# Linear attention and a SoLU feed-forward on one core: chunk 0 in token halves, and an order of work read from a table

## The chip, the cores and the metric

The kernel runs on one core of a Trainium2 chip. The metric is device microseconds of one execution, from which the median of several runs is taken. Profiles are of one further execution by the hardware profiler; their span runs from the first to the last instruction. PE is TensorE, DVE VectorE, ACT ScalarE, POOL GpSimd, SP SyncE.

## What is computed

For 8 batches of 8 heads, 576 tokens and 64 columns per head (fp32 inputs), linear attention without a softmax, then a root-mean-square norm per head; then a feed-forward with 512 inputs, 1024 hidden columns and a SoLU (h times its softmax, layer-normed):

```python
kv = np.einsum('bhsd,bhse->bhde', k, v)
out = np.einsum('bhsd,bhde->bhse', q, kv)
rms = np.sqrt(np.mean(out * out, axis=-1, keepdims=True) + 1e-06)
x = (out / rms * g_norm)          # heads side by side: 4608 tokens x 512
h = x @ w_in
sm = softmax(h)                   # over the 1024 columns, +1e-9 in the sum
solu = h * sm
ln = (solu - mean(solu)) / np.sqrt(var(solu) + 1e-06) * g_ln
return ln @ w_out                 # 4608 x 512, fp32
```

## The kernel before, in words

**Chunks.** The 4608 tokens go in nine chunks of 512. Chunk c below 8 holds tokens 0 to 7 of each run of nine tokens of batch c (a batch is 64 partitions by nine tokens); chunk 8 holds the ninth token of all eight batches, for which q_last (L235) is loaded.

**Attention of a chunk.** k, v and q are cast to bf16 by loads from POOL's queue (L225). For batches 0 and 1 each load is cut into two halves of heads, for the others it is whole. kv_mm (L279) forms k'v on PE, copies put it into kvd in two row arrangements (L298). q is transposed on PE (qT_mm, L312, and a copy) for chunks 0 to 3, and by a DMA transpose from SP's queue for chunks 4 to 8 (q_turn, L329). o_mm (L336) gives q times kv in two PSUM tiles; each is squared (o_sq L360, for one tile of chunk 0 a DVE copy and a POOL product, L352 to L358), averaged over the head on PE (s_mm, L366), turned into 1/rms on ACT (in chunk 0 by a reciprocal square root, L380; later by Ln and Exp, L370 and L374, in another table of ACT functions, loaded once at L394), and multiplied in (x_mul, L386). So a chunk has four quarters (half hf, tile z); in the kernel before, half hf of chunk 0 means four of the eight heads.

**Feed-forward of a chunk.** h_mm (L466) makes eight groups of four matmuls with 512 columns, one per 128 hidden columns; each needs all four quarters of x. Exp goes to ACT (L474), u = h times exp to DVE (L481), u squared to POOL or ACT (u_sq, L488), the sum of two exps to POOL (e_sum, L497). sums (L526) adds u, u squared and the exps over the hidden columns on PE; a transpose and a few small DVE operations and two of ACT give one factor per token (rstd, L558). out_mm (L579) multiplies u by w_out, which is first centred (w_mean L565, w_center L573), in four token blocks of two groups; scale (L613) applies the factor, store (L626) writes out. In chunk 8 the last block is cut into two halves of columns (L588 to L611), and each block is stored by two DMAs of 64 rows.

**Order.** Every piece of work is given to Plan (L19) with an engine, a length, a rank, what it needs, and the buffers that it opens and uses; order (L42) then picks, again and again, the piece that could start first by these lengths, the lower rank first. This fixes each engine's instruction order; on the chip every engine works its list strictly in order. PSUM's eight banks are dealt into five pools that rotate (L136): two for h, two for out, two for o, one for s, one for the rest. Engines are fixed by rules (for instance L295, L515, L615). POOL's loads of batches 5 to 7 wait in the plan until the transpose of the batch before has been given out ("turned", L256), and the plan charges a transpose that meets a busy load queue 12.0 instead of 3.5 (L81 to L84):

```python
if n[0] == "qT" and engine == "sp":

    if queue > t - 2.0:
        length, queue = 12.0, queue + 2.2
```

At most eight DMAs of POOL's queue are outstanding; the next one waits for the one eight places earlier. Matmuls on zeros (warm, L207) fill PE's first 18 us.

## Time and profile before

| what | value |
|---|---|
| median of 3 runs | 192.51 us (192.28 to 195.38) |
| span of the profiled execution | 191.5 us |
| PE busy | 178.6 us, 93% of the span |
| ACT, POOL, DVE busy | 141.2, 128.5, 122.5 us |
| granted TensorE clock, mean | 0.998 |
| loads on POOL's queue | 17.30 MB written, q0 |
| stores and transposes, SP's and ACT's queues | 11.68 MB, q1 |

The timeline lists instructions in the order of time: start, duration, engine, line, operation, destination <- sources, and in brackets how long the engine idled before it and what ended that. A row may merge several of the same kind (x4). Matmul durations contain the pipeline, so that rows overlap: a group of four is listed with about 1.03 us and occupies 0.86. A row of SP, ACTq or POOL with DMA in it is the issue of the transfer, not the transfer.

### The profile page before, as it was taken

Reading aid. Unit: us, or ns where it says so; the run is one execution under the profiler, and the core shown is the slowest. Engines: PE = TensorE matmul, PEld = TensorE weight load, DVE = VectorE, ACT = ScalarE, POOL = GpSimd, SP = SyncE. Lnnn points to the kernel's source line nnn. Section 1 sums busy time; section 2 is a strip of 40 time slices with the busy share of each in tenths; the row PEclk is TensorE's granted clock in tenths of the full one; section 3 lists DMA queues with packets and bytes.
Section 4 is the critical chain, followed back from the end, with each engine's and each line's share of the span. In section 5 each row is a group of like instructions: output and inputs, shape, how many; then the busy total and the mean of one; then the engine's idle time right before and its main releaser. Section 6 shows DMA issues by size and latency. Waiting matters only on the chain.

```text
span 191.5 us, 5356 instructions
## 1 busy us (share of the span) xinstructions
PE 178.6 (93%) x2218; PEld 88.5 (46%) x2218; DVE 122.5 (64%) x241; ACT 141.2 (74%) x245; POOL 128.5 (67%) x136
## 2 busy tenths in 40 slices
PE   7989796999799999999999999999999999999980
PEld 2343355554245554554455446445444544544550
DVE  1445679386866878577686758586676847565350
ACT  2026897879898899989888897989787796555330
POOL 7953499600799886796897996698387646854200
PEclk9999999999999999999999999999999999999999
DMA  3999999999995599699999999448824022414435
GB/s 49 179 197 259 364 208 209 204 209 258 249 207 86 119 167 249 168 178 229 219 152 232 243 149 174 107 49 159 98 55 103 14 55 68 99 33 96 93 74 145
DMA packets 35607, 29.70 MB, mean 155 GB/s; under 512 B 16504, under 2 KB 30080, under 8 KB 35584
## 3 DMA queue, kind: packets, MB, share of 16 engines
q0 software_dynamic: 19088, 17.30, 54.9%
q1 hardware_dynamic: 16176, 11.68, 26.8%
q10 hardware_dynamic: 320, 0.39, 0.6%
q8 instruction: 17, 0.28, 0.6%
q14 instruction: 6, 0.05, 0.1%
HBM read 32.51 MB, written 9.44 MB: 219 GB/s over the span
## 4 chain that ended last, share of the span: by engine, by line
PE 72%; DMA 11%; POOL 5%; ACT 5%; DVE 3%; issue 1%; ACTq 1%; POOLq 0%
PE out_ps L583 28%; PE h_ps L469 28%; DMA v_sb<-in_v_dram 11%; PE misc_ps L535 5%; PE s_ps L368 3%; PE o_ps L347 2%; POOL usq_sb L495 2%; DVE x_sb L389 2%; ACT rst_sb L376 2%; PE misc_ps L290 1%; POOL k_sb L230 1%; ACT lss_sb L372 1%; PE misc_ps L210 1%; DVE u_sb L484 1%; PE o_ps L583 1%
## 5 line engine op out<-in xcount | busy, mean ns | idle before, releaser
L469 PE MATMUL h_ps<-x_sb,w_in_sb 128*128 128x512 bf16 x276 | 70.5, 379 | 2.3 <-DVE x_sb L389 1.1
L583 PE MATMUL out_ps<-w_out_sb,u_sb 128*128 128x512 bf16 x272 | 69.4, 379 | 0.0
L495 POOL TENSOR_TENSOR usq_sb<-u_sb 128x512 bf16<-128x512 bf16 x50 | 51.8, 1041 | 23.0 <-DVE u_sb L484 22.9
L484 DVE TENSOR_TENSOR u_sb<-h_ps,e_sb 128x512 bf16<-128x512 f32 x69 | 47.4, 687 | 25.7 <-ACT e_sb L477 24.9
L501 POOL TENSOR_TENSOR es_sb<-e_sb 128x512 bf16<-128x512 f32 x36 | 45.8, 1274 | 19.7 <-ACT e_sb L477 19.4
L477 ACT ACTIVATE e_sb<-h_ps,zero_t 128x512 f32<-128x512 f32 x69 | 47.0, 681 | 9.2 <-PE h_ps L469 8.7
L469 PEld LDWEIGHTS <-w_in_sb 128*128 128x128 bf16 x288 | 27.0, 98 | 35.6 <-issue 5.4
L583 PEld LDWEIGHTS <-u_sb 128*128 128x128 bf16 x280 | 26.4, 98 | 31.2 <-issue 1.0
L389 DVE SCALAR_TENSOR_TENSOR x_sb<-o_ps,g_rep,rst_sb 128x512 bf16<-128x512 f32 x32 | 23.9, 748 | 11.6 <-ACT rst_sb L376 11.6
L618 DVE TENSOR_SCALAR ob_sb<-out_ps,rstd 128x512 f32<-128x512 f32 x33 | 24.6, 746 | 6.9 <-PE out_ps L583 4.4
L362 ACT ACTIVATE osq_sb<-o_ps,zero_t 128x512 bf16<-128x512 f32 x31 | 20.0, 680 | 12.2 <-PE o_ps L347 12.2
L372 ACT ACTIVATE lss_sb<-s_ps,eps_t 128x512 f32<-128x512 f32 x32 | 22.1, 689 | 2.4 <-PE s_ps L368 2.3
L376 ACT ACTIVATE rst_sb<-lss_sb,zero_t 128x512 f32<-128x512 f32 x32 | 23.1, 723 | 0.8
L493 ACT ACTIVATE usq_sb<-u_sb,zero_t 128x512 bf16<-128x512 bf16 x22 | 15.8, 718 | 9.1 <-DVE u_sb L484 9.0
L368 PE MATMUL s_ps<-osq_sb,head_mean 128*128 128x512 bf16 x34 | 12.9, 379 | 0.6 <-ACT osq_sb L362 0.6
L535 PEld LDWEIGHTS <-stat_sel 128*32 128x32 bf16 x720 | 10.1, 97 | 3.8 <-issue 3.8
L210 PE MATMUL s_ps<-zeros 128*128 128x512 bf16 x28 | 10.1, 488 | 1.4 <-DVE zero_t L175 1.2
L230 POOL DMA_DIRECT2D k_sb<-in_k_dram x10 | 7.7, 773 | 4.3 <-DMA w_in_sb<-in_moe_w_in_dram 2.8
L230 POOL DMA_DIRECT2D q_sb<-in_q_dram x10 | 7.5, 750 | 3.6 <-DMA w_in_sb<-in_moe_w_in_dram 1.4
L308 DVE CAST kvd<-misc_ps 64x128 bf16<-64x128 f32 (+1 forms) x24 | 6.9, 288 | 3.2 <-PE misc_ps L290 2.0
L290 PEld LDWEIGHTS <-k_sb 64*64 64x64 bf16 x576 | 7.5, 107 | 3.2 <-issue 3.2
L290 PE MATMUL misc_ps<-v_sb,k_sb 64*64 64x64 bf16 x360 | 7.8, 194 | 1.0 <-DMA v_sb<-in_v_dram 0.9
(85 smaller groups left out, 132.6 us busy)
## 6 DMA issues: line engine op xcount, KB each, us to landing
out_dram<-ob_sb SPq DMA_DIRECT2D x68, 128.0 KB, 3.1
k_sb<-in_k_dram POOLq DMA_DIRECT2D x6, 576.0 KB, 12.3
v_sb<-in_v_dram POOLq DMA_DIRECT2D x6, 576.0 KB, 12.6
q_sb<-in_q_dram POOLq DMA_DIRECT2D x6, 512.0 KB, 14.3
w_out_f<-in_moe_w_out_dram POOLq DMA_DIRECT2D x1, 2048.0 KB, 17.4
k_sb<-in_k_dram POOLq DMA_DIRECT2D x4, 288.0 KB, 12.4
v_sb<-in_v_dram POOLq DMA_DIRECT2D x4, 288.0 KB, 12.6
q_sb<-in_q_dram POOLq DMA_DIRECT2D x4, 256.0 KB, 12.5
```

The source lines that it names most:

```text
L362: nc.scalar.activation(out=t[:, :], in_=T[("o", *i)].rearrange("p a b c -> p (a b c)"), func=AF.Square, bias=zero_t[:, :])
L372: nc.scalar.activation(out=t[:, :], in_=T["s", i][:, :], func=AF.Ln, bias=eps_t[:, :])
L376: nc.scalar.activation(out=t.rearrange("p a b c -> p (a b c)"), in_=T["lss", i][:, :], func=AF.Exp, scale=-0.5, bias=zero_t[:, :])
L389: nc.vector.scalar_tensor_tensor(out=T["x", c][:, 2 * hf:2 * hf + 2, z], in0=T["o", c, hf, z][:, :, :, :], scalar=g_rep[:, :], in1=T["rst" ...
L469: nc.tensor.matmul(t[:, :], w_in_sb[:, dt, f * 128:(f + 1) * 128], T["x", c][:, dt].rearrange("p a b c -> p (a b c)"), start=(dt == 0), st ...
L477: nc.scalar.activation(out=T["e", c, f // 2][:, f % 2, :], in_=T["h", c, f][:, :], func=AF.Exp, bias=zero_t[:, :])
L484: nc.vector.tensor_tensor(out=T["u", c][:, f, :], in0=T["h", c, f][:, :], in1=T["e", c, f // 2][:, f % 2, :], op=MUL)
L495: nc.gpsimd.tensor_tensor(out=dst, in0=src, in1=src, op=MUL)
L501: nc.gpsimd.tensor_tensor(out=T["es", c][:, n, :], in0=e[:, 0, :], in1=e[:, 1, :], op=ADD)
L535: nc.tensor.matmul(T["sum", c][32 * j:32 * j + 32, 0, :], stat_sel[:, i, :], cols, start=(part == 0 and n == 0), stop=(part == 2 and n == ...
L583: nc.tensor.matmul(T["acc", c, m][:, :], T["u", c][:, f, m * 128:(m + 1) * 128], w_out_sb[:, f, :], start=(f == 0), stop=(f == NF - 1),)
L618: nc.vector.tensor_scalar_mul(out=t[:, :], in0=T["acc", c, m][:, :], scalar1=T["rstd", c][:, m:m + 1])
```

## The change

1. **An order from a table.** Plan no longer schedules. A string, ORDER, lists all pieces; each entry may name the engine (`@act`) and the slots of the buffers that the piece opens (`=2`). The eight PSUM banks become one pool, `ps`, any bank for any tile. The fused o_mm and kv_mm of the old plan are gone.
2. **Chunk 0 in halves of its tokens.** For chunk 0, half hf now means half of each head's tokens, for all heads: q of batch 0 is loaded in two token halves, transposes and o_mm go by token half (16 shorter matmuls instead of 8 per half), and h_mm, exp and u of chunk 0 are cut into 16 pieces of 256 columns; a piece needs two quarters of x instead of four.
3. **Last tokens placed for stores of 128 rows.** The batches of q_last are placed so that a block's 128 rows are two neighbouring batches, one DMA per block (and per column half in the last block).

```diff
+ORDER = """
+warm.0=7 v.0.0=0 k.0.0=0 warm.1=7 warm.2=7 kv_mm.0.0=0 kv.0.0.0@act kv.0.0.1@act kv.0.0.2@act k.0.1 v.0.1 warm.3=7
...
+    def emit(self, order):
...
+             fn(engine or engines[0])
...
-    banks = {"h": 2, "out": 2, "o": 2, "s": 1, "misc": 1}
...
+        "ps": 8, "k": 3, "v": 3, "q": 3, "qT": 3, "osq": 4, "lss": 2, "rst": 3, "oc": 1, "x": 2, "e": 4, "u": 2, "usq": 2,
...
+        if parts > 1 and (name, b) == ("q", 0):
+            at = slice(4 * part, 4 * part + 4)
...
-        behind = [] if b < 2 else [("h_mm", 0, 0)] if b == 2 else [("h_mm", b - 3, 2 if b == 3 else 0)] + ([("turned", b - 1)] if b - 1 in XBAR else [])
...
+    def h_mm(c, f, g):
+        t = T["h", c, f, g] = bank(("ps", "h", c, f, g), [128, 512 if g is None else 256], FP32)
+        for dt in range(NP):
+            nc.tensor.matmul(
+                t[:, :], w_in_sb[:, dt, f * 128:(f + 1) * 128], T["x", c][:, dt, cols_of(g)],
+                start=(dt == 0), stop=(dt == NP - 1),
+            )
...
+    def last_rows(m):
+        a = 4 * (m % 2) + 2 * (m // 2)
+        return out.rearrange("(b p j) d -> j (b p) d", p=64, j=9)[8, 64 * a:64 * a + 128]
...
+    def store(engine, c, m):
+        if c == NC - 1:
+            of(engine).dma_start(last_rows(m), T["ob", c, m][:, :])
+            return
```

The table's entries, sorted by engine, in the places that matter below (piece.chunk.part):

```text
POOL  v.0.0 k.0.0 k.0.1 v.0.1 ident q.0.0 q.0.1 w_in.0 w_in.1 w_out sq.0.0.1 k.1.0 q.1.0 v.1.0 v.1.1 k.1.1
      q.1.1 k.2.0 usq.0.0 usq.0.3 usq.0.6 usq.0.1 usq.0.2 es.0.0 usq.0.5 usq.0.4 v.2.0 q.2.0 es.0.2 es.0.3
      usq.0.7 es.0.1 k.3.0 v.3.0 q_last.3 q_last.0 q.3.0 v.4.0 k.4.0 usq.1.0 usq.1.2 q.4.0 v.5.0 q.5.0 k.6.0
      q_last.6 es.1.0 es.1.2 es.1.3 usq.1.1 es.1.1 v.6.0 usq.1.7 usq.1.5 usq.2.0 usq.1.4 usq.2.2 k.5.0 ...
PE    ... s_mm.0.1.1 h_mm.0.3.0 h_mm.0.0.0 h_mm.0.2.0 h_mm.0.1.0 h_mm.0.4.0 h_mm.0.4.1 h_mm.0.0.1 h_mm.0.6.0
      h_mm.0.2.1 ... h_mm.0.5.1 w_mean qT_mm.1.0 kv_mm.1.0 o_mm.1.0 out.0.1.0 ... sums.0 kv_mm.2.0 h_mm.1.0 ...
      out.1.0.0 out.1.2.1 o_mm.4.0 out.1.0.1 h_mm.3.0 ... h_mm.3.5 kv_mm.5.0 o_mm.4.1 sums.2 ...
      out.8.1.0 sums.8 out.8.1.1 out.8.2.1 out.8.0.1 out.8.3.1
ACT   ... ex.0.1.1 table exp.0.0.0 ... sq.2.0.1 sq.2.0.0 sq.2.1.1 sq.2.1.0 ln.2.0.0 ln.2.0.1 ex.2.0.0 ex.2.0.1
      ln.2.1.0 ln.2.1.1 ex.2.1.0 ex.2.1.1 exp.1.4 exp.1.3 exp.1.5 exp.1.7 ...
      rstd.8 ob.8.3.0 ob.8.0 store.8.0 store.8.1
SP    store.0.2 store.0.0 qT.4 store.0.3 store.0.1 store.1.3 qT.5 ... store.8.3.0 store.8.2 store.8.3.1
```

## The prediction

> **What bounds the kernel now.** I read the page first: busy shares, then the 40 slices.

> ```profile
> span 191.5 us, 5356 instructions
> ...
> PE 178.6 (93%) x2218; PEld 88.5 (46%) x2218; DVE 122.5 (64%) x241; ACT 141.2 (74%) x245; POOL 128.5 (67%) x136
> ...
> PE   7989796999799999999999999999999999999980
> ...
> DMA  3999999999995599699999999448824022414435
> ```

> A slice is 4.8 us. PE is the bound from slice 13 (about 60 us) to slice 38 (184 us); there its busy time fills every window, so the order of its work is worth nothing there. Gains can only lie in the first 60 us, where DMA is full as well, and behind the last matmul. So I read PE's order of time up to 60 us.

> ```profile
> 12.81 0.76 PE L290 MATMUL misc_ps<-v_sb,k_sb 64*64 64x64 bf16 x36 [0.53 <-DMA v_sb<-in_v_dram]
> ...
> 14.16 0.62 PE L318 MATMUL h_ps<-ident,q_sb 128*128 128x128 bf16 x8 [0.27 <-DMA q_sb<-in_q_dram]
> ...
> 20.28 1.46 PE L469 MATMUL h_ps<-x_sb,w_in_sb 128*128 128x512 bf16 x6 [1.13 <-DVE x_sb L389]
> ...
> 25.70 2.21 PE L568 MATMUL out_ps<-w_out_f,g_mean 128*128 128x512 f32 x8
> 27.75 1.04 PE L469 MATMUL h_ps<-x_sb,w_in_sb 128*128 128x512 bf16 x4
> 28.72 0.76 PE L290 MATMUL misc_ps<-v_sb,k_sb 64*64 64x64 bf16 x36
> 30.37 0.61 PE L318 MATMUL misc_ps<-ident,q_sb 128*128 128x128 bf16 x8 [0.90 <-ACT kvd L310]
> ...
> 49.23 2.13 PE L469 MATMUL h_ps<-x_sb,w_in_sb 128*128 128x512 bf16 x8 [0.97 <-DVE u_sb L484]
> ```

> The reader is to see: the up-projection h starts at 20.28, behind x; then waits of up to 1 us until 50. A group of four 512-column matmuls takes 0.863 us (1.73 for eight in the chain). Last the end of the timeline, and SP's queue:

> ```profile
> 184.06 1.91 PE L593 MATMUL h_ps<-w_out_sb,u_sb 128*128 128x256 bf16 x16
> ...
> 186.38 0.47 ACT L604 ACTIVATE ob_sb<-h_ps,rstd 128x256 f32<-128x256 f32 x1 [1.39 <-PE h_ps L593]
> 186.63 1.19 SPq L609 DMA_DIRECT2D out_dram<-ob_sb  x2
> 186.88 1.23 ACTq L609 DMA_DIRECT2D out_dram<-ob_sb  x2
> ```

> ```profile
> 61.38 1.73 SPq L332 DMA_TRANSPOSE qT_sb<-q_sb  x1
> ...
> 80.04 2.83 SPq L332 DMA_TRANSPOSE qT_sb<-q_sb  x1
> ```

> PE ends at 185.97 and 5.5 us follow it. The median of the runs, 192.51, is 1.0 above the profiled span; the sum is made on the span, and 1.0 is added.

> **The change, part by part.** I walk the table by hand, each engine in its new order, with durations of rows.

> *Start, to 27.8 us.* k and v of batch 0 now precede q. Between 12.81 and 14.16 landed q's second half, 0.52 MB of fp32 source: 390 GB/s. k and v complete 0.52 MB earlier, 11.5; the first token half of q lands at 12.8, the second at 14.15 as now. (Its rows are half as long; no row shows the price. Ends: 0 and one such load, 1.3 us; I take 0, since the bytes are the same.) The chain for token half 0: transposes 13.2, copy 0.69 to 14.4, o_mm to 14.9 (16 short matmuls for 8: 32 of them in o_mm of the last chunk take 0.38 where 8 take 0.34, so under 0.1 more), DVE copy 0.69 to 15.6, POOL square 1.05 to 16.7, s_mm 0.39, ACT's rsqrt, behind a square, to 18.1, x 0.75 to 18.85. So h starts at 18.9, 1.4 earlier, and eight banks take eight half groups ahead of any exp. But ACT must finish all four rsqrt (19.9) and the table load (1.28) first: its first exp is at 21.2, where it now is at 20.91. A 256-column ACT operation is 0.473 against 0.687 (L604, L616); from the 0.57 pitch of full ones that leaves 0.36, 16 of them to 26.9. A half group of matmuls is 0.43, so PE is done with h at 25.8; 8 more exps and 8 more u cost ACT and DVE 1.2 us each, hidden, as five squares of 0.72 leave ACT. The w_out mean waits for w_out (landed 25.7) and ends at 27.8, as now. Now one h group is still owed there: **gain 0.9**.

> *27.8 to 41.* Chunk 1's q and v halves land at 28.1 and 29.65 (same bytes in another order; now q is there at 29.6). PE holds only transposes, kv_mm and o_mm ahead of the next out group, so it idles about 2.2 us to 31.2; the page's kernel idles 2.0 between 28 and 40. **0.** k1 moves on POOL from 8.99 to behind the square at 16.7: w_in and w_out keep the DMA queue full until 25.7, so 0; without that cover 1 to 2 us. POOL gets five squares of chunk 0 more (5.0 us), and v2 and q2 are issued behind eight POOL operations, at 32 instead of 25.8; k2 occupies the DMA queue until 36.6. es.0.1, the last input of sums.0, ends at 38.0, and PE asks at 38.6: hidden by 0.6.

> *41 to 90.* PE now idles 2.6 here. From 41.5 (the same state of work, with two s_mm owed, as the table's 40.6) to 93.3 it does 43 groups (37.1), 4 transposes (1.8), 6 o_mm (2.0), 3 kv_mm (2.1), 12 s_mm (2.6), 2 sums (2.5) and switches (1.1): 49.2 in 51.8. In the walk the table finds no wait here but one: **gain 2.6**. The closest places are x of chunk 2 (53.7, wanted at 53.8) and k5 (75 to 80, wanted at 81): if the first gives way, all of chunk 2's h queues behind it on PE, and ACT and DVE wait for that.

> *The one wait.* Now POOL's loads of batch 5 are held until transposed q4 is issued, and DMA is empty at 61. The table issues v5, q5 and k6 before, by 52, and v6 by 60. q4 lands at about 61.4 (61.38 now: two loads of last tokens more ahead of it, four stores fewer); SP then issues its transpose into full queues, and in PE's order o_mm.4.0 comes at 71.2, with out.1.0.1 and all h of chunk 3 behind it. Rows: 3.8 us to landing in the empty queue, 7.7 for the one at 80.04, whose later half met k6's load. Doubling that extra 3.9 gives 11.6; the old planner writes 12.0 for a busy queue. Ends: no wait (anything up to 9.8), and 6.1 (landing only after 4.7 MB of loads have drained, 12.1 us, plus 3.8). I take 11.0, as some packets get through first: **loss 1.2**. [...]

> *90 to the end.* All that is left is PE work in the same amount, in the full stretch: 0. The table gives ACT 17 squares instead of 22 and 13 output scales instead of 2, some 15 us of work per chunk beside PE's 17; if a chunk's exp came late all the same, PE would wait with everything behind it, for which I allow 0 to 1 in the range. At the end sums.8 is wanted about 3.5 us before PE's end; POOL's last chain (es.8.3, es.8.1, a square, es.8.2: 1.27, 1.27, 1.04, 1.27 from the last exp) is done within half a microsecond of that: **loss 0.2** (0 to 1). Behind the last matmul: one DVE scale 0.49, one store issue instead of two (0.6 saved), 2.8 to landing, and ACT's last store issued 0.6 behind another: 4.8 against 5.5, **gain 0.7**. The 128-row stores save 5 issues of 10; only this last one counts.

> Sum: 191.5 - 0.9 - 2.6 + 1.2 + 0.2 - 0.7 = 188.7, and 1.0 around it: 189.7 us.

> **The rivals.**

> *No wait for the transpose.* The DMA engines serve it at once, landing within 9.8 us; for it speaks the 7.7 row, against it that loads covered only part of that. Then 189.7 - 1.2 - 0.2 = 188.3.

> *Slower: transposed q4 is held until the loads drain.* One in-order place, o_mm.4.0. It lands at 77.3, or 80.3 if k5 (issued at 66) goes first: PE waits 6.1 to 9.1, and 188.3 becomes 194.4 to 197.4. It decides from a wait of 4.2 on (gains 0.9 + 2.6 + 0.7). Against it speaks that the 7.7 row was partly beside k6's load and still landed before k6 did (87.7, 88.3). So it gets 0.08. [...]

> *ACT keeps the old waits.* The table puts chunk 2's four squares, ln and exp ahead of four of chunk 1's exps, and ACT is full from 45 to 56. x of chunk 2 has 0.1 to spare. If ACT runs 1.5 to 2 late there, most of the 2.6 is gone: about 191.4. For it speaks ACT's 4.97 of 5 us in the window from 45 to 50 now; against it, that PE has out groups between.

> **How the numbers follow.** Forecast (wait of 0.7 to 2.5) 0.45, no wait 0.30, ACT 0.17, drained 0.08. The likeliest is 189.7, its own range 189.0 to 191.2. The range of 8 in 10 runs from 187.0 (no wait, and the DMA early by 1) to 193.0 (ACT's case and a longer wait). About 2% is what a measurement of this kernel can tell from no change: 188.66 and 196.36. Faster: the no-wait case and a little of the forecast, 0.36; slower by more: most of the drained case, 0.06; within: 0.58.

> **What would show it.** First h matmul at 18.9 and first exp at 21.2; the w_out mean's end at 27.8; PE idle about 2 us from 28 to 31; no PE wait over 0.3 from 41 to 60; the transpose of q4 landing 9 to 12 us after an issue near 61, and PE waiting for it about 1 us near 71; sums.8 within 0.5 of es.8.2; 4.8 us behind the last matmul. I am wrong if q or w_out land elsewhere than their bytes say, if ACT shows waiting exps and PE idles near 54, or if PE waits in the stretch from 90 to 180 at all, where I priced the new order at nothing.

## The result, and the profile after

| kernel | median of its runs, us | against before |
|---|---|---|
| before | 193.58 (192.28 to 195.38, 4 runs) | 1 |
| changed | 205.16 (204.48 to 205.74, 4 runs) | 1.064 (95%: 1.056 to 1.072) |

The changed kernel is 6.4% slower; forecast were 189.7 us and a range up to 193.0. The profiled execution has a span of 203.7 us. In later comparisons the median contains a few slow runs; the ratios leave them out, so ratios are what is compared there.

The page of the changed kernel, its first lines and its 40 slices (5.1 us each here):

```profile
span 203.7 us, 5452 instructions
...
PE 178.6 (88%) x2241; PEld 92.2 (45%) x2263; DVE 116.2 (57%) x242; ACT 141.9 (70%) x255; POOL 132.9 (65%) x141
...
PE   7787989899999901998499999999999999999991
...
PEclk9999999999999995599889999999999999999998
DMA  4999999999999999998826882297420233406175
```

PE has the same busy time as before, 178.6 us, in a span 12.2 longer. The loss lies in two places: slices 15 and 16 (from 71 us) and slice 20 (from 97), and PEclk falls behind each. Before, that row held nines throughout. DMA is full to slice 18; before, it had a pause in slices 13 and 14. PE's rows in the order of time:

```profile
19.09 7.15 PE L489 MATMUL h_ps<-x_sb,w_in_sb 128*128 128x256 bf16 x64
25.99 2.11 PE L584 MATMUL mean_ps<-w_out_f,g_mean 128*128 128x512 f32 x8
...
41.02 0.47 PE L326 MATMUL kv_ps<-v_sb,k_sb 64*64 64x64 bf16 x35 [0.94 <-issue]
...
80.81 0.64 PE L372 MATMUL o_ps<-qT_sb,kvd 64*64 64x256 bf16 x8 [9.04 <-DMA qT_sb<-q_sb]
81.38 1.89 PE L596 MATMUL out_ps<-w_out_sb,u_sb 128*128 128x512 bf16 x4
83.06 3.62 PE L489 MATMUL h_ps<-x_sb,w_in_sb 128*128 128x512 bf16 x8
...
99.56 0.35 PE L553 MATMUL sum_ps<-es_sb,stat_sel 128*32 128x128 bf16 x11 [3.48 <-issue]
```

To be seen: the start is as forecast (h at 19.09, the w_out mean through by 27.9). PE reaches o_mm.4.0 at 71.8 and waits 9.04 us for the transpose; out.1.0.1, which stands next in the table and takes nothing from it, starts behind it at 81.38. The groups behind that wait take twice their time: 1.89 us for four matmuls that elsewhere take 1.03. Then PE stops in the middle of sums.2, between the fifth and the sixth matmul of one row, and the releaser is "issue": no semaphore, no transfer, nothing that the profile shows. The chain that ended last says the same:

```profile
62.37 18.39 DMA qT_sb<-q_sb
...
94.97 1.11 PE sum_ps L553 x69
96.08 3.48 issue
```

The clock is read from stretches of the timeline (start:end, length, busy time of PE, PEld, DVE, ACT and POOL, then PEclk, DMA share, GB/s):

```profile
72.00:76.00 4.00, 0.00 (x0) 0.00 (x0) 1.87 (x3) 0.29 (x1) 3.87 (x5) 1.00 1.31 152
76.00:77.00 1.00, 0.00 (x0) 0.00 (x0) 0.00 (x0) 0.00 (x0) 0.00 (x0) 0.68 1.22 200
77.00:80.00 3.00, 0.00 (x0) 0.00 (x0) 0.00 (x0) 0.00 (x0) 0.00 (x0) 0.50 1.20 197
80.00:86.00 6.00, 5.19 (x19) 1.84 (x20) 0.95 (x2) 1.95 (x3) 0.00 (x0) 0.50 1.25 246
86.00:87.00 1.00, 1.00 (x5) 0.43 (x4) 0.49 (x1) 0.04 (x1) 0.43 (x1) 0.70 1.43 91
```

The granted clock falls to 0.50 about 4.6 us into the idle time and stays there to 86.6, 5.8 us past the first matmul: some 2.8 us of work lost beside the wait. Behind the stop at 96.08 it is 0.50 again:

```profile
100.50:103.00 2.50, 2.50 (x7) 0.87 (x6) 0.34 (x3) 1.18 (x3) 2.50 (x3) 0.50 0.77 125
```

With the parts before and behind (0.88 from 99.5 to 100.5, 0.67 from 103 to 104) that is 3.4 us at half clock, about 1.7 us of work.

The sum, from the forecast for the profiled execution, 188.7: less the wait of 1.2 and the 0.2 at sums.8 that it held, 187.3; 0.6 for reaching o_mm.4.0 at 71.8 instead of 71.2; 9.0 for the wait, 2.8 for its clock, 3.5 for the stop, 1.7 for its clock; 0.4 less at the tail: 204.5, against 203.7 measured.

### The profile page after: what moved, and what is told of

It is laid out like the page before. It is cut to its first block, busy times and chain, and to the rows that moved or that the text cites. A ratio compares the mean times of both kernels' runs of the same rounds, so it can differ in the third digit from the quotient of the medians.

```text
span 203.7 us, 5452 instructions
## 1 busy us (share of the span) xinstructions
PE 178.6 (88%) x2241; PEld 92.2 (45%) x2263; DVE 116.2 (57%) x242; ACT 141.9 (70%) x255; POOL 132.9 (65%) x141
## 4 chain that ended last, share of the span: by engine, by line
PE 77%; DMA 12%; DVE 4%; issue 4%; ACT 1%; POOL 0%; POOLq 0%
PE h_ps L489 30%; PE out_ps L596 28%; DMA qT_sb<-q_sb 9%; PE sum_ps L553 5%; PE kv_ps L326 3%; PE s_ps L394 3%; PE o_ps L372 3%; DMA k_sb<-in_k_dram 3%; DVE w_out_sb L587 2%; PE warm_ps L246 2%; DVE qT_sb L191 1%; PE qT_ps L347 1%; PE mean_ps L584 1%; PE acc_ps L605 1%; ACT osq_sb L388 1%
## 5 line engine op out<-in xcount | busy, mean ns | idle before, releaser
L515 POOL TENSOR_TENSOR usq_sb<-u_sb 128x512 bf16<-128x512 bf16 x55 | 56.3, 1039 | 36.7 <-DVE u_sb L504 36.6
L489 PE MATMUL h_ps<-x_sb,w_in_sb 128*128 128x512 bf16 (+1 forms) x313 | 67.5, 364 | 0.5 <-issue 0.2
L504 DVE TENSOR_TENSOR u_sb<-h_ps,e_sb 128x512 bf16<-128x512 f32 (+1 forms) x80 | 48.2, 633 | 25.3 <-ACT e_sb L497 24.5
L497 ACT ACTIVATE e_sb<-h_ps,zero_t 128x512 f32<-128x512 f32 (+1 forms) x80 | 48.0, 650 | 15.3 <-PE h_ps L489 14.3
L388 ACT ACTIVATE osq_sb<-o_ps,zero_t 128x512 bf16<-128x512 f32 x35 | 22.4, 684 | 11.6 <-PE o_ps L372 11.4
L613 DVE TENSOR_SCALAR ob_sb<-out_ps,rstd 128x512 f32<-128x512 f32 x23 | 16.7, 745 | 11.5 <-DMA out_dram<-ob_sb 8.6
L372 PE MATMUL o_ps<-qT_sb,kvd 64*64 64x256 bf16 (+2 forms) x208 | 7.6, 249 | 11.1 <-DMA qT_sb<-q_sb 9.0
L191 DVE CAST kvd<-kv_ps 64x128 bf16<-64x128 f32 (+1 forms) x27 | 7.7, 288 | 11.9 <-PE kv_ps L326 11.4
L189 ACT CAST kvd<-kv_ps 64x128 bf16<-64x128 f32 (+1 forms) x21 | 5.4, 260 | 10.8 <-PE kv_ps L326 6.8
L246 PE MATMUL warm_ps<-zeros 128*128 128x512 bf16 x32 | 10.4, 443 | 1.8 <-DVE zeros L210 1.2
L513 ACT ACTIVATE usq_sb<-u_sb,zero_t 128x512 bf16<-128x512 bf16 x17 | 11.8, 715 | 0.0
L326 PE MATMUL kv_ps<-v_sb,k_sb 64*64 64x64 bf16 x576 | 8.0, 194 | 1.7 <-issue 0.9
## 6 DMA issues: line engine op xcount, KB each, us to landing
v_sb<-in_v_dram POOLq DMA_DIRECT2D x6, 576.0 KB, 14.4
```

The source lines that it names most:

```text
L388: nc.scalar.activation(out=t[:, :], in_=T[("o", *i)].rearrange("p a b c -> p (a b c)"), func=AF.Square, bias=zero_t[:, :])
L489: nc.tensor.matmul(t[:, :], w_in_sb[:, dt, f * 128:(f + 1) * 128], T["x", c][:, dt, cols_of(g)], start=(dt == 0), stop=(dt == NP - 1),)
L497: nc.scalar.activation(out=T["e", c, f // 2][:, f % 2, cols_of(g)], in_=T["h", c, f, g][:, :], func=AF.Exp, bias=zero_t[:, :])
L504: nc.vector.tensor_tensor(out=T["u", c][:, f, cols_of(g)], in0=T["h", c, f, g][:, :], in1=T["e", c, f // 2][:, f % 2, cols_of(g)], op=MUL)
L515: of(engine).tensor_tensor(out=dst, in0=src, in1=src, op=MUL)
```

## The experiments

Theory one: loads ahead of it in the DMA queues hold transposed q4 back, in its strict form until they are through (draining). Theory two: PE stops when it comes to the end of a block of its instructions before the next block is there. Theory three: a PE that stood still works on at half clock, so that each wait costs more than itself.

**Loads behind the transpose (e1: all five; e2: three of them), or no DMA transpose (e4).** The edit of e1 in the table; for e2 v.5.0 and q.5.0 stay where they were:

```diff
-v.5.0=2 q.5.0=2 k.6.0=2 q_last.6
...
-v.6.0=0
...
+v.5.0=2 k.5.0=0 q.5.0=2
...
+k.6.0=2 v.6.0=0 v.7.0=1 q_last.4 q_last.6
```

e4 leaves the loads early and lets PE turn chunk 4's q:

```diff
-qT.4=1
...
+qT_mm.4.0=0 qT_mm.4.1=6 qT.4.0@dve=1 qT.4.1@dve
...
-    XBAR = tuple(range(4, NC))
+    XBAR = tuple(range(5, NC))
```

Expected of e1:

> Only the five loads of batches 5 and 6 that the table issued at 50 to 60 us are moved behind the issue of transposed q4 (to about 66 to 72 us). Theory (the transpose of q4 is held back by loads that stand in the DMA queues ahead of it): it lands 4 to 8 us after its issue near 62, before PE asks at 71.8, so the 9.0 us wait and the 10 us at half clock (2.8 us) both go: 203.7 - 9.0 - 2.8 = about 192 for the profiled execution, 188 if the later 3.5 us stop at sums.2 with its half clock goes as well. Rival (a transpose in this place is slow for a reason of its own, whatever the loads do): it lands 15 to 18 us after its issue again, the wait stays near 9 and the time near 204. Second rival (late loads only move the wait): PE waits for k5, v5 or q5 near 85 to 95 and 2 to 9 us come back there.

Expected of e2:

> Half the dose: batch 5's v and q stay at 50 us, only k6, v6 and the last tokens of q6 are moved behind the transpose. Loads ahead of the transpose at 62.4: about 2.1 MB instead of 4.7, by 390 GB/s 5.4 us. Theory of draining (the transpose goes on when what was issued ahead of it is through): it lands at 68 to 72, PE waits 0 to 0.5 us, time as with all loads late. Theory of turns (it gets a fixed small share while any load is there; 1404 packets in 18.4 us were 76 per us): it has 410 packets at 68 and k5, issued at 66, keeps it slow until 70 and the loads behind after that: it lands at 74 to 80, PE waits 2 to 8 us.

Expected of e4:

> Chunk 4's q is transposed by TensorE with a copy on VectorE, as chunks 0 to 3 are, and the loads stay early. No DMA transpose is wanted before qT.5 near 100. Theory: the wait of 9.0 and the half clock of 2.8 go, and 8 short transposes and a pass of two copies come in (1.2 us on PE): 203.7 - 9.0 - 2.8 + 1.2 = about 193; 188 to 190 if the stop at sums.2 goes too. Rival (early loads themselves slow this stretch, through the stores or k5): PE waits for something else between 72 and 90, and the time stays above 197.

Measured: e1 201.12 us (ratio 1.045, 1.043 to 1.048; span 199.5), e2 one run of 195.93 (span 193.9), e4 194.14 (1.013, 1.005 to 1.021; span 192.1). The transpose issued near 62.4, with the time to its landing (issues of that microsecond, count, us), in the changed kernel, in e2 and in e1:

```profile
qT_sb<-q_sb SPq DMA_TRANSPOSE x1, 18.4
```

```profile
qT_sb<-q_sb SPq DMA_TRANSPOSE x1, 9.2
```

```profile
qT_sb<-q_sb SPq DMA_TRANSPOSE x1, 3.7
```

So the loads are what holds it back: with none ahead it lands after 3.7 us, with v5 and q5 issued ahead (2.2 MB of fp32 source) after 9.2, with 4.7 MB after 18.4, and the wait of 9 us is gone in all three runs. e4 came out near its 193, though its interval leaves open whether it is 2% slower than before.

How the loads hold it back is read from the packets (queue, packets, MB, share of the span of the 16 engines). q0 has the loads, q1 the transposes and stores. The changed kernel from 62 to 66 us, where q1 has no packet, and from 67 to 81:

```profile
q0 software_dynamic: 782, 0.81, 121.4%
```

```profile
q0 software_dynamic: 2089, 1.81, 88.5%
q1 hardware_dynamic: 2097, 0.66, 40.3%
```

The first packet of the transpose starts at 66.4, 4.0 us after the issue. From there the two queues move packet for packet: 2048 packets of the transpose beside 2117 of loads, in 13.9 us; the landing follows 0.5 us later, 18.4 in all. In the kernel before, with no load beside it, the transpose issued at 61.38 had its first packet after 1.3 us and moved its 2048 in 2.0. e3 has them one for one as well: from 74 to 80 us 741 packets of q1 beside 740 of q0. So it was not draining: v6, issued ahead of the transpose at 60.2, landed at 78.4, 12.0 us behind the transpose's first packet, and k5, issued at 66.0, landed at 82.7, behind the transpose. In e2 the transpose, issued at 62.62, landed at 71.8, in the 68 to 72 that the draining theory gave, while the theory of turns missed with 74 to 80. The first theory holds for the cause, not for its strict form. What keeps the first packet back for 4.0 us, against 1.3 before, is open.

The pace in e2's theory of turns, 76 packets per us, was too low: the changed kernel's transpose had 147 per us beside loads (2048 in 13.9 us). The 1404 packets behind the 76 are those of q1 from 131 to 134 us in the kernel before, a window that ended before its transpose did; to 137 it has 2112 small packets, 2048 of them of 256 bytes. With an even share for each of the 16 engines, 128 packets, the 13.9 us are an estimated 108 ns per packet and the load packet beside it.

But e1 missed its 188 to 192: the stop grew to 6.11 us, PE waited 2.06 us for ACT ahead of it, and the granted clock was 0.50 from 86.5 to 100.2. The second rival of e1, a wait for k5, v5 or q5, did not come up. PE's rows of e1, then of e2:

```profile
85.16 0.76 PE L326 MATMUL kv_ps<-v_sb,k_sb 64*64 64x64 bf16 x70 [2.06 <-ACT lss_sb L398]
...
94.69 0.51 PE L553 MATMUL sum_ps<-es_sb,stat_sel 128*32 128x128 bf16 x11 [6.11 <-issue]
```

```profile
72.09 0.41 PE L372 MATMUL o_ps<-qT_sb,kvd 64*64 64x256 bf16 x8
...
89.91 0.44 PE L553 MATMUL sum_ps<-es_sb,stat_sel 128*32 128x128 bf16 x11 [4.11 <-issue]
```

In all three kernels PE stops at the same matmul, the sixth of that row, at 96, 89 and 86 us. In e4, whose 16 transposes stand ahead of it, the stop has moved back inside sums.2, and a second one has come:

```profile
87.41 0.35 PE L554 MATMUL sum_ps<-usq_sb,stat_sel 128*32 128x128 bf16 x11 [0.72 <-issue]
...
106.95 0.26 PE L327 MATMUL kv_ps<-v_sb,k_sb 64*64 64x64 bf16 x8 [1.59 <-issue]
```

Counted in the program (a matmul as two instructions, its weight load and itself; the page of the changed kernel lists 2263 and 2241 of them), both cases are TensorE's instruction 2214, the 1115th matmul. The count starts 16 instructions late, the same in all kernels; only the distances between its numbers are used.

**Matmuls in the wait (e3).** Nothing but work on zeros:

```diff
-qT.4=1 store.0.3 o_mm.4.0=06
+qT.4=1 store.0.3 warm.12=6 o_mm.4.0=06
```

Expected of e3:

> 40 matmuls on zeros into a free bank stand before o_mm.4.0, in the wait; nothing else is changed. Theory (the 4.7 us without a matmul made the clock fall to half, and that cost 2.8 us beside the wait): the wait for the transpose still ends near 80.8, the granted clock stays at 1.0 from 72 to 90, and the time falls by 2.5 to 3, to about 201 for the profiled execution. Rival (the clock fell for another reason, or the half clock was hidden by other waits): time within 0.7 us of the changed kernel, 203 to 204.5.

Measured: 201.13 us (1.046, 1.040 to 1.053), span 200.9, 2.8 below the changed kernel's. The wait is filled and the clock holds:

```profile
72.53 8.80 PE L246 MATMUL warm_ps<-zeros 128*128 128x512 bf16 x40
81.26 0.54 PE L372 MATMUL o_ps<-qT_sb,kvd 64*64 64x256 bf16 x8
```

```profile
76.00:80.00 4.00, 4.00 (x20) 1.85 (x19) 0.00 (x0) 0.00 (x0) 0.84 (x1) 1.00 1.20 213
80.00:84.00 4.00, 4.00 (x26) 1.73 (x24) 0.75 (x1) 1.54 (x3) 0.00 (x0) 1.00 1.15 276
```

The size is as expected but not clean: the 40 matmuls also shifted the instruction numbers, the stop at sums.2 went, and three others came (0.49, 1.52 and 1.47 us). That the clock holds at 1.00 where it was 0.50, with the transpose landing near 80 as before, is what carries the third theory. In the changed kernel the clock fell 4.6 us into the idle time; in f2, below, it fell in an idle time of 2.07 us.

**Where PE stops.** All stops of over 0.4 us in the profiles of before, of the changed kernel and of e1 to e4, with the work in the 256 instructions before (counts from the program, durations from rows: 216 ns for a 512-column matmul, 43 for one of o_mm, 14 for one of sums, 8 for one of kv_mm):

| instruction | kernel: work of the block, stop (us) |
|---|---|
| 938 | changed, e2 3.82, 0.94; e1 3.82, 0.65; e3 3.82, 0.67; e4 3.82, 1.03 |
| 2214 | changed 1.75, 3.48; e2 1.75, 4.11; e1 1.75, 6.11; e4 1.65, 0.72; e3 5.45, none |
| 2724 | e3 1.82, 0.49; e4 1.67, 1.59; changed 3.23, none |
| 3234 | e3 1.74, 1.52; changed 7.43, none |
| 4002 | e3 1.62, 1.47; changed 8.25, none |
| before, shortest block | 3.99, none |

The numbers are 1276, 510, 510 and 768 apart: 5, 2, 2 and 3 times 256, less at most four. With the semaphore instructions that the changed kernel's trace lists among them (5, 2, 2 and none) counted too, the distances are 1281, 512, 512 and 768. Every stop lies at the end of a block with 1.62 to 3.82 us of work, whatever the instructions are; one block of 3.23 has none, and no block of 3.99 or more has one. Queue q8, which the page calls instruction, moved 17 packets of 16 KB before and 17 in the changed kernel; that they hold TensorE's instructions is an estimate, from 4504 of these in the changed kernel's page, 265 to a packet. One started at 97.3 in the changed kernel, 87.5 to 88.0 in e2 and 85.0 to 85.5 in e4, and PE went on 2.3 us later in the first and 1.9 to 2.4 later in the other two (in e1 2.7 to 3.2 us behind one at 91.5 to 92.0).

**Shifting the numbers (f1: e2; f2: the changed kernel; f3: e4).** The first warm-up becomes shorter matmuls, 72 more (f3: 60), in the same time:

```diff
-            nc.tensor.matmul(t[:, :], zeros[:, 0:128], zeros[:, :], start=True, stop=True)
+            nc.tensor.matmul(t[:, 0:w], zeros[:, 0:128], zeros[:, 0:w], start=True, stop=True)
...
+        w = 64 if n > 2 else 512
...
-        plan.add(("warm", i), "pe", lambda _, i=i: warm(("ps", "warm", i), 2 if i else 12), first=[("ps", "warm", i)])
+        plan.add(("warm", i), "pe", lambda _, i=i: warm(("ps", "warm", i), 2 if i else 84), first=[("ps", "warm", i)])
```

Expected of f1:

> e2 (half the loads late) plus 72 more instruction pairs at the very start: the first twelve warm-up matmuls of 512 columns become 84 of 64 columns, about the same time, and every later TensorE instruction has a number higher by 144. In the runs so far PE stopped with nothing to wait for at TensorE instructions 938, 2214, 2724, 3234 and 4002 of the program, whatever stood there: multiples of 256 (less one or two) from each other, and only where the 256 before took under 4 us. Theory (PE runs through a 16 KB block of instructions before the next one has arrived): with the shift the shortest block takes 4.2 us instead of 1.75, so the stops of 0.94 and 4.11 us and the half clock behind (about 1.6) go: 193.9 - 6.6 = 187.3 for the profiled execution, to 188.5 if one stop of 1.2 comes at the block of 4.2. Rival (the stop belongs to sums.2, its inputs or its PSUM bank): it stays at sums.2 with 3 to 6 us and the time stays at 193 to 196.

Expected of f2:

> The changed kernel with the 144 instructions more at the start and nothing else; the loads stay early. Theory: the wait for transposed q4 (9.0 us) and its half clock (2.8) stay, the stops of 0.94 and 3.48 and the half clock behind (1.5) go: 203.7 - 5.9 = 197.8 for the profiled execution. Rival (the stop belongs to sums.2 or is an after-effect of the first wait): no change, 203 to 205.

Expected of f3:

> e4 (chunk 4's q transposed on TensorE, loads early) with 60 more instruction pairs in the warm-up: the shortest block takes 4.5 us instead of 1.65. Theory: the stops of 1.03, 0.72 and 1.59 go: 192.1 - 3.3 = 188.8 for the profiled execution. Rival (stops move to other places and cost the same in sum): 191 to 193.

Measured: f1 189.98 us, ratio 0.984 (0.982 to 0.987), span 188.6; f2 200.93 (1.044, 1.038 to 1.051), span 200.3; f3 192.50 (0.999, 0.995 to 1.002), span 191.3. In none of the three is a stop on "issue" left. sums.2 of f1 runs through:

```profile
82.34 0.78 PE L327 MATMUL kv_ps<-v_sb,k_sb 64*64 64x64 bf16 x72
82.93 0.41 PE L373 MATMUL o_ps<-qT_sb,kvd 64*64 64x256 bf16 x8
83.35 0.63 PE L554 MATMUL sum_ps<-u_sb,stat_sel 128*32 128x128 bf16 x32
83.79 0.63 PE L554 MATMUL sum_ps<-usq_sb,stat_sel 128*32 128x128 bf16 x32
84.24 0.41 PE L554 MATMUL sum_ps<-es_sb,stat_sel 128*32 128x128 bf16 x16
```

So the stops went when the instruction numbers were shifted, and the one at 96 us did not belong to sums.2. That PE waits for its next block, as the second theory says, is the author's reading of the distances and of the 16 KB packets above; no trace names what the stops wait for. f1 has only three loads and, by the shorter warm-up matmuls, the instruction numbers changed; it came out near its 187.3 to 188.5 and is 1.6% faster than before. f2 keeps the wait (8.87 us), as it should, and missed its 197.8 by 2.5 for a reason of the shift itself: the shorter warm-up ended early, PE idled 2.07 us before the first keys, and the clock fell there too.

```profile
8.89 1.17 PE L327 MATMUL kv_ps<-v_sb,k_sb 64*64 64x64 bf16 x36 [2.07 <-DMA k_sb<-in_k_dram]
...
83.25 0.64 PE L373 MATMUL o_ps<-qT_sb,kvd 64*64 64x256 bf16 x8 [8.87 <-DMA qT_sb<-q_sb]
```

```profile
8.00:9.00 1.00, 0.11 (x4) 0.11 (x6) 0.00 (x0) 0.00 (x0) 1.00 (x2) 0.71 1.16 183
10.00:14.00 4.00, 3.89 (x12) 1.07 (x9) 0.00 (x0) 0.78 (x3) 0.00 (x0) 0.50 1.36 192
```

Its first o_mm came at 18.37 instead of 14.60; less that 3.8, f2 is at 196.5. f3 missed its 188.8 in the same way: PE idled 1.65 us there, the granted clock was 0.69 in the mean from 10 to 15 us, and the start was 2.0 us late; less that it is at 189.3. Yet in g3, below, PE idled 2.14 us in the same place and the clock stayed at 1.00, so idle times of about 2 us do not settle it.

**Longer warm-up matmuls (g1, g2, g3).** 80 columns instead of 64, for f1, for e1 with the shift, and for f3:

```diff
-        w = 64 if n > 2 else 512
+        w = 80 if n > 2 else 512
```

Expected of g1:

> As f1 (half the loads late, TensorE's instruction numbers 144 higher), with warm-up matmuls of 80 columns instead of 64. In f2 and f3 the shorter ones were through early, TensorE idled 2.07 and 1.65 us before the first keys (f1: 0.76), the granted clock fell to 0.5, and the first o_mm came 3.5 and 2.0 us later. Theory: with the longer ones that idle time is under 1 us, the start does not vary, and the profiled execution takes 188 to 189, the median 189 to 190, 1.5% less than before in every round. Rival (the start varies for a reason of the loads): executions 2 to 3.5 us slower come again.

Expected of g2:

> e1 (all five loads behind the transpose) with the same 144 instructions more. Theory (all that e1 lost after the transpose was cured was the stop of 6.11, the one of 0.65, the half clock behind them, 3 us, and ACT's 2 us before kv_mm): 199.5 - 9.8 = about 189.7 for the profiled execution; 188 if the wait for ACT goes too. Rival (late loads bring a wait of their own, for k, v or q of batches 5 and 6): 192 or more, with a wait for a load between 75 and 100 us.

Expected of g3:

> f3 (chunk 4's q transposed on TensorE, loads early, no stops) with warm-up matmuls of 80 columns. Theory: f3's profiled 191.3 less the 2.0 us of its late start, 189.3, and a median near 190.5; with the loads early and nothing held back by them it is within 1 us of g1. Rival (early loads cost something beside the transpose): 191 or more.

Measured: g1 0.988 (0.982 to 0.994), span 188.0; g2 1.001 (0.999 to 1.003), g3 0.995 (0.991 to 0.999). No stop in any of them. g1 is faster than before again, but no steadier than f1 (its interval is 0.012 wide, that of f1 0.005) and short of its 1.5%, so the width was not the reason: the first keys were there at 8.62 us in g1 and at 7.92 in f1, and the start varies with that. g2 missed its 189.7. It has no stop and no wait for a load in its profile between 75 and 100, but a wait of 2.88 for a scale on VectorE near 97; f1 has the same wait with 0.94, and the profiled execution of g2 was above its median. Whether that is the cause was not settled, and so it stays open why all five loads late are worth less than three. g3 missed too (0.995, where its 190.5 would be 0.990 of before). In its profile, also of an execution above the median, PE waits 2.24 us for keys near 62; whether that is a price of the early loads, as its rival has it, was not tested.

## Why the prediction was wrong

- **The start: right.** h was forecast at 18.9 and came at 19.09, the first exp at 21.2 and came at 21.20, the w_out mean's end at 27.8 and came near 27.9.
- **27.8 to 41, and 41 to 71: right but for one stop.** PE idled 0.95 and 0.29 for data, less than the 2.2 forecast up to 31.2, and 0.94 on instructions, and reached o_mm.4.0 at 71.8 instead of 71.2. No wait for ACT over 0.3 came up, so that rival falls. f1 shows the gains: the whole order with two disturbances taken out is 1.6% faster than before.
- **The one wait: wrong, and this decided it.** The step took the landing at 11.0 us, "as some packets get through first"; it was 18.4, and the wait 9.04 instead of 1.2. That packets get through beside the loads was right; the pace was not: 2048 packets took 13.9 us instead of 2.0, and 4.0 passed before the first. The 3.9 that the step doubled came from a row of 7.7 us that had almost no load beside it: from 80 to 84 us 1526 packets of q1 moved and none of q0. The rival in which the transpose is held until the loads drain had 194.4 to 197.4 for waits of 6.1 to 9.1 and got 0.08. Its landing at 80.3 is close to the 80.77 measured, but that is luck: the loads had not drained, and k5, which was to go first, landed behind it.
- **What a wait costs: left out.** In each term a wait of n us was charged n. A wait of 9.0 cost 11.8 and a stop of 3.5 cost 5.2, since the granted clock was 0.50 for the 5.8 us of work behind the wait and for about 3.4 us behind the stop.
- **"90 to the end ... 0": wrong by one mechanism that was not in the list, though a PE wait in this stretch was named as a sign of being wrong.** The amount of PE work was right (178.6 in both), and behind 104 us PE is full but for some tenths. The stop at 96 belongs to the order: kv_mm.5.0, o_mm.4.1 and sums.2 stand back to back, 160 short matmuls, of which 149 took 2.1 us, and an end of the blocks counted above falls among them. The old order had no block under 3.99 us at such an end. The distances between stops agree with blocks of 256 instructions; one stop cost up to 6.11 us (e1).
- **The tail: right.** 4.4 us from the end of the last matmul to the end of the span, forecast 4.8, 5.5 before; sums.8 did not wait.

Had the drain been taken as the forecast, the time would have been 197.4 at most; the other 8 us are the two clock losses (4.5) and the stop (3.5).

## What to carry to other kernels

Look at what the load queue holds when a DMA transpose that something waits for is issued: here its 2048 packets took 2.0 us with no load beside them and 13.9 beside 2117 packets of loads. A gate that holds loads back until such a transfer is issued is part of the schedule and must be kept when an order is written out as a table. Count a wait on TensorE with the work at the lower clock that the trace shows behind it (2.8 us behind the wait of 9.04). Where many short matmuls stand together, look at which instruction a stop lies: if stops come at a fixed number and not at a fixed operation, as here, move the numbers (no stop was left in f1 to f3), or spread the short ones between long ones, which no run here tried.
